# Zero fills of an attention-backward kernel as casting copies from an fp8 tile, issued by GpSimd

## The chip, the cores and the metric

The kernel runs on one core of a Trainium2 chip. The metric is the device time of one execution in microseconds (us). Engines are named as in the profile: PE is TensorE, DVE is VectorE, ACT is ScalarE, POOL is GpSimd and SP is SyncE. DMA transfers are carried by 16 DMA engines that all issuing engines share.

## The reference

One decode step of a transformer block and its gradients. A query of one token attends to the last 4096 of 32768 cached positions; the outputs hold the forward result and the gradients with regard to every input, the two whole caches among them.

```python
W = min(4096, max(256, Sk // 4))            # Sk = 32768: W = 4096
q = (x @ wq)                                # 16 heads of 256, 8 key/value heads
k = jnp.repeat(k_cache[:, :, Sk - W:, :], rep, axis=1)
v = jnp.repeat(v_cache[:, :, Sk - W:, :], rep, axis=1)
p = _softmax(jnp.einsum("bhqd,bhkd->bhqk", q, k) * (Dh ** -0.5), axis=-1)
a = jnp.einsum("bhqk,bhkd->bhqd", p, v)     # then @ wo
...
h = x + A(layernorm(x)); h2 = h + ((n @ w_gate) * (n @ w_up)) @ w_down   # n = layernorm(h)
...
_out, _vjp = jax.vjp(_f, A_x, A_k_cache, A_v_cache, A_wq, A_wo, B_w_gate, B_w_up, B_w_down)
```

The gradients of the caches (`out_2` for K, `out_3` for V) have the caches' shape, 8 x 32768 x 256 in bf16. Only the last 4096 positions of each head have a gradient; the other 28672 are zero, and the kernel has to write these zeros: 14.68 MB for each of 8 heads and 2 outputs, 234.9 MB in all.

## The kernel before, in words

The kernel is written with a tile framework that inserts the semaphores and chooses the order of the instructions on each engine; the order on an engine is fixed when the program is built, and each engine works its instructions off in that order. Two names choose the engine that issues transfers: `FILL` (SP before the change) for the zero fills and for the rows `x` and `grad_out`, and `IO` (POOL before the change) for all other loads and stores. The framework gives the transfers of each kind of issuer eight semaphores in turn, so a transfer that takes a semaphore again waits on its issuing engine until the one eight before it has landed.

The fills (lines 57 to 62): a tile `zeros` of 128 x 8192 bf16, 16 KB per partition, is cleared once by DVE, and 16 transfers copy it seven times each to the zero region of one head of one output, 128 x 7 rows of 16 KB.

The rest is one long chain of stages in which PE, DVE and ACT take part.

- Constants: POOL builds the two identity matrices `ident_bf` and `ident_f`, then `Par`, `Ed` and `Eq`. From `ident_f`, DVE works out `par`, `msk` (lines 112 to 117) and `mrow`.
- Head: `x` is put into columns and normalised; the normalised vector is multiplied with `msk` to give `xx` (line 188); 112 matmuls with `wq` (line 227) give `q`.
- Phase 1, eight groups g (lines 348 to 366), one per key/value head: load K and V of the window (`load_K`, `load_V`, line 79), scores with PE transposes (line 266), softmax, and `moments` (lines 308 to 334), whose matmuls need V and write to `MT` and `acc`. K and V lie in eight slots of 2 MB of one tile `S`; a load into a slot waits for the last reader of what was there. The first slots hold `wq`, so V loads into them wait for q.
- Middle: `wo` is loaded in two halves (`woA` at line 360, ahead of V of the last group's load in the queue; `woB` at line 375), `ao` is summed (line 382), then the gate and up projections, the second layernorm, the gradients down to `doT`, `dq_ps` (line 452) and `dq_bc`.
- Phase 2, eight groups g again (from line 559 on): V is transposed (line 567), `dp` is formed, and 32 matmuls per group (`d_ps`, line 601) give the gradient rows of V and K for the window. ACT and DVE take turns to copy them to staging slots of `S` (`evac`, lines 210 and 212), and two transfers of 2 MB per group store them (line 606). Between the groups stand side jobs: the outer products of the weight gradients (`outer`, lines 470 to 476), which DVE writes to two staging buffers in `Mt` and POOL stores, and the second reading of `wq` (lines 507 and 511).

Transfers of rows of 448 bf16 (896 B): `w_down` twice, `wo`, and the stores of the gradients of `wo` and `w_down`. All other large transfers on `IO` have rows of 2 KB and more.

Of the kernel before, what the change touches and what calls it, by code (L numbers as in the profile page):

```python
# [6 lines left out]

bf16 = mybir.dt.bfloat16
f32 = mybir.dt.float32
AX = mybir.AxisListType.X  # L10
ALU = mybir.AluOpType
ACT = mybir.ActivationFunctionType

D = 448
# [3 lines left out]
Dh = 256  # L18
W = 4096
# [3 lines left out]
Sk = 32768  # L23
# [4 lines left out]
NV = 5  # L28
HQ = H * Dh // 2
HF = F // 2  # L30
ZW = 8192
NZ = (Sk - W) * Dh // (128 * ZW)


K_SLOT = [5, 6, 7, 5, 6, 7, 5, 7]
# [5 lines left out]
def kernel(  # L41
        ctx, tc, A_x, A_k_cache, A_v_cache, A_wq, A_wo, B_x, B_w_gate, B_w_up, B_w_down, grad_out,
           out_0, out_1, out_2, out_3, out_4, out_5, out_6, out_7, out_8):
    nc = tc.nc
    V_, S_, P_ = nc.vector, nc.scalar, nc.tensor
    FILL = nc.sync
    IO = nc.gpsimd

    const = ctx.enter_context(tc.tile_pool(name="const", bufs=1))
    small = ctx.enter_context(tc.tile_pool(name="small", bufs=2))  # L50
    ps = ctx.enter_context(tc.tile_pool(name="ps", bufs=1, space=bass.MemoryType.PSUM))

    x_bf = const.tile([1, D], bf16, tag="rowa", name="x_bf")
    FILL.dma_start(out=x_bf[:], in_=A_x.rearrange("a b d -> (a b) d"))
    go_bf = const.tile([1, D], bf16, tag="rowb", name="go_bf")
    FILL.dma_start(out=go_bf[:], in_=grad_out.rearrange("a b d -> (a b) d"))
    zeros = const.tile([128, ZW], bf16)
    V_.memset(zeros[:], 0.0)
    for g in range(G):
        for o in (out_2, out_3):  # L60
            reg = o[0, g, 0:Sk - W, :].rearrange("s d -> (s d)").rearrange("(p n f) -> p n f", p=128, f=ZW)
            FILL.dma_start(out=reg, in_=zeros[:].unsqueeze(1).to_broadcast([128, NZ, ZW]))


    S = const.tile([128, NS, SLOT], bf16)
# [12 lines left out]
    def load_window(dst, cache, g):  # L78
        IO.dma_start(out=dst, in_=cache[0, g, Sk - W:, :].rearrange("(p t) d -> p t d", t=T))

    def load_K(g):
        load_window(Kw[g], A_k_cache, g)

    def load_V(g):
        load_window(Vw[g], A_v_cache, g)

    def flat_rows(w):
        return w.rearrange("a b -> (a b)").rearrange("(p x) -> p x", p=128)


    wq_sb = S[:, 1:3, :].rearrange("p a b -> p (a b)")[:, 0:NI * HQ]
    IO.dma_start(out=wq_sb, in_=flat_rows(A_wq))
    load_K(0)
    load_V(0)
    load_K(1)
    wd0 = S[:, 3, 0:FC * D].rearrange("p (c n) -> p c n", n=D)
    IO.dma_start(out=wd0, in_=B_w_down.rearrange("(c p) n -> p c n", p=128))

# [12 lines left out]
    par = const.tile([128, 2], f32)  # L111
    V_.reduce_sum(out=par[:, 1:2], in_=ident_f[:, 1::2], axis=AX)
    V_.tensor_scalar(out=par[:, 0:1], in0=par[:, 1:2], scalar1=-1.0, scalar2=1.0, op0=ALU.mult, op1=ALU.add)
# [54 lines left out]
    def layernorm(X, tag):  # L168
        s1 = small.tile([128, 1], f32, tag="ln_s")
        V_.reduce_sum(out=s1[:], in_=X, axis=AX)  # L170
        nm = small.tile([128, 1], f32, tag="ln_nm")
# [19 lines left out]
    def layernorm_bwd(Pp, xh, rstd, extra, gain, tag):  # L191

        st = small.tile([128, 2], f32, tag="lb_st")
        V_.reduce_sum(out=st[:, 0:1], in_=Pp, axis=AX)
        jk = small.tile([128, NI], f32, tag="lb_j")
# [87 lines left out]
    def softmax(g):  # L283
        s = sT[g]
        pmax = small.tile([128, 2], f32, tag="pmax")
        V_.reduce_max(out=pmax[:], in_=s[:].rearrange("p t h -> p h t"), axis=AX)
        mt = ps.tile([2, 128], f32, tag="tmp", bufs=1)
        P_.transpose(mt[:], pmax[:], ident_f[:])
        gmax = small.tile([2, 1], f32, tag="gmax")
        V_.reduce_max(out=gmax[:], in_=mt[:], axis=AX)  # L290
        gd = small.tile([2, 2], f32, tag="gd")
        V_.tensor_scalar(out=gd[:], in0=ident_f[0:2, 0:2], scalar1=gmax[:, 0:1], scalar2=-SCALE, op0=ALU.mult, op1=ALU.mult)
        nb = ps.tile([128, 2], f32, tag="tmp", bufs=1)
        P_.matmul(nb[:], lhsT=ones_f[0:2, :], rhs=gd[:], start=True, stop=True)
        nbias = small.tile([128, 2], f32, tag="nbias")
        V_.tensor_copy(out=nbias[:], in_=nb[:])
        e = small.tile([128, T, 2], f32, tag="e_f")
        sums = small.tile([128, 2], f32, tag="psums")
        for h in range(2):
            S_.activation(out=e[:, :, h], in_=s[:, :, h], func=ACT.Exp, bias=nbias[:, h:h + 1], scale=SCALE, accum_out=sums[:, h:h + 1])  # L300
        rs = small.tile([128, 2], f32, tag="rsum")
        V_.reciprocal(out=rs[:], in_=total(sums[:], 2)[:])
        pf = small.tile([128, T, 2], f32, tag="p_f")
        V_.tensor_tensor(out=pf[:], in0=e[:], in1=rs[:].unsqueeze(1).to_broadcast([128, T, 2]), op=ALU.mult)
        V_.tensor_copy(out=pT_all[:, g], in_=pf[:])
        p_f[g] = pf
# [41 lines left out]
    for g in range(G):  # L348
# [9 lines left out]
        if g == 7:  # L358
            load_V(7)
            IO.dma_start(out=woA, in_=wo_v[:, 0:16, :])  # L360
        softmax(g)
# [5 lines left out]
        if g == 0:  # L367
# [4 lines left out]
            for c in range(FC):  # L372
                V_.tensor_tensor_reduce(out=wd0[:, c, :], in0=wd0[:, c, :], in1=dh2_bc[:], scale=1.0, scalar=0.0,
                                        op0=ALU.mult, op1=ALU.add, accum_out=d_hh[:, c:c + 1])
    IO.dma_start(out=woB, in_=wo_v[:, 16:32, :])
    IO.dma_start(out=wg_sb, in_=flat_rows(B_w_gate))
    IO.dma_start(out=wu_sb, in_=flat_rows(B_w_up))
# [62 lines left out]
    pd = small.tile([128, H], f32, tag="pd")  # L440
    V_.reduce_sum(out=pd[:], in_=od[:].rearrange("p (h f) -> p h f", f=2), axis=AX)
    delta = const.tile([128, H], f32)
# [108 lines left out]
    rowb = late[:, 14336:16384].rearrange("p (k a c) -> p k a c", k=2, a=8)  # L551
# [7 lines left out]
    for g in range(G):  # L559
# [36 lines left out]
        for c in range(T // 2):  # L596
            d_ps = bps.tile([128, 2, 2, Dh], f32, tag="d2", bufs=2)
            for i in range(2):
                t = 2 * c + i
                k, a = t // 8, t % 8  # L600
# [38 lines left out]
```

## Time and profile before

| What | Value |
|---|---|
| time, median of 2 runs | 814.19 us (814.14 to 814.24) |
| span of the profiled execution | 812.7 us |
| bytes moved by DMA | 338.58 MB |
| HBM read, written | 57.28 MB, 280.59 MB |
| PE busy | 495.5 us (61%) |
| DVE busy | 374.0 us (46%) |
| ACT busy | 164.7 us (20%) |
| POOL busy | 40.5 us (5%) |
| q1 (SP's transfers) | 234.88 MB |
| q0 (POOL's transfers) | 103.00 MB |

How to read it: the span runs from the first to the last instruction of one profiled execution, and the medians come from runs of their own. Busy shares are averages over stages that differ. A row of 40 digits cuts the span in 40 equal slices (20.3 us each here), and a digit is a busy share in tenths, 9 for 90% and more. In a timeline line the first number is the start and the second the duration in us, then engine, line, operation, what is written and what is read; a bracket gives the idle time of the engine before it and what ended that. In a line of waits the numbers are the total in us, how often, and the longest. In the chain of waits each piece is start, duration and what the time was spent on.

### The profile page before, as it was taken

The page shows a single profiled execution, that of the slowest core. Times are in us where ns is not written, and L with a number is a line of the kernel's source. Part 1 is how long each engine was busy: PE and PEld are TensorE (multiplying, and loading weights), DVE is VectorE, ACT ScalarE, POOL GpSimd, SP SyncE. Part 2 cuts the span into 40 slices and gives each one's busy share as a digit, 9 for nine tenths or more (in the row PEclk, how much of TensorE's full clock was granted, in tenths as well). Part 3 has the DMA queues.
Part 4 walks back from the last instruction along what each step waited for, and adds up shares of the span by engine and source line. Part 5 has one row for each costly group of instructions (what it writes and reads, how often), then busy time and mean ns, then how long its engine had stood idle before and what let it go on. Part 6 is the DMA issues. An engine that isn't in the chain of part 4 may idle for free.

```text
span 812.7 us, 10923 instructions
## 1 busy us (share of the span) xinstructions
PE 495.5 (61%) x4479; PEld 289.6 (36%) x4479; DVE 374.0 (46%) x1149; ACT 164.7 (20%) x261; POOL 40.5 (5%) x75
## 2 busy tenths in 40 slices
PE   3559949999647519035497576099759674554500
PEld 3545636666223405013495432044325331210100
DVE  4128727777445306005671455366455435352500
ACT  0230101222000200001001233044435342332300
POOL 3000000000000001000000100001000001000000
PEclk9959778999678758655556555555555555555555
DMA  8999999999999999999999999999999999999994
GB/s 344 427 426 429 427 433 424 432 424 429 431 422 431 418 429 429 409 430 429 427 427 433 423 410 418 430 428 417 424 406 429 424 418 419 420 427 422 427 427 187
DMA packets 24567, 338.58 MB, mean 417 GB/s; under 512 B 1251, under 2 KB 1317, under 8 KB 4677
## 3 DMA queue, kind: packets, MB, share of 16 engines
q1 hardware_dynamic: 14596, 234.88, 68.4%
q0 software_dynamic: 9920, 103.00, 30.3%
q8 instruction: 35, 0.57, 0.3%
q14 instruction: 16, 0.12, 0.0%
HBM read 57.28 MB, written 280.59 MB: 416 GB/s over the span
## 4 chain that ended last, share of the span: by engine, by line
issue 29%; DMA 16%; PE 11%; DVE 4%; POOL 2%; ACT 1%; POOLq 0%; DVEq 0%
DMA S<-in_A_v_cache_dram 4%; DMA S<-in_A_wo_dram 4%; DMA Rt<-in_A_wq_dram 4%; DMA out_dram<-Mt 3%; PE dq_ps L452 3%; PE MT L322 2%; POOL out_dram L476 1%; DVE Rt L422 1%; POOL out_dram L606 1%; PE dh_ps L159 1%; PE d_ps L601 1%; PE tr L567 1%; PE t L412 1%; PE ao L382 1%; DVE Rt L511 1%
## 5 line engine op out<-in xcount | busy, mean ns | idle before, releaser
L601 PE MATMUL d_ps<-R,Mt 32*128 32x512 bf16 x256 | 124.4, 613 | 92.4 <-DVE S L212 91.6
L322 PE MATMUL MT<-Rt,S 128*128 128x512 bf16 x512 | 145.9, 397 | 30.7 <-DMA S<-in_A_v_cache_dram 29.8
L318 DVE TENSOR_SCALAR Rt<-S,pf 128x256 bf16<-128x256 bf16 x512 | 117.0, 281 | 56.4 <-PE MT L322 49.7
L212 DVE CAST S<-d_ps 128x512 bf16<-128x512 f32 x128 | 86.7, 688 | 55.5 <-ACT S L210 44.0
L210 ACT CAST S<-d_ps 128x512 bf16<-128x512 f32 x128 | 75.0, 586 | 169.8 <-PE d_ps L601 169.8
L601 PEld LDWEIGHTS <-Mt 32*128 32x128 bf16 x256 | 23.3, 114 | 146.1 <-issue 144.7
L567 PE MATMUL tr<-ident_bf,S 128*128 128x128 bf16 x512 | 69.6, 306 | 3.5 <-ACT Mt L210 3.5
L325 PEld LDWEIGHTS <-S 128*128 128x128 bf16 x512 | 49.4, 100 | 60.9 <-issue 9.5
L266 PE MATMUL tr<-ident_bf,S 128*128 128x128 bf16 x512 | 48.6, 253 | 36.4 <-DMA S<-in_A_k_cache_dram 32.0
L567 PEld LDWEIGHTS <-S 128*128 128x128 bf16 x512 | 49.2, 137 | 28.0 <-issue 27.8
L266 PEld LDWEIGHTS <-S 128*128 128x128 bf16 x512 | 38.1, 115 | 34.7 <-DMA S<-in_A_k_cache_dram 32.3
L325 PE MATMUL acc<-pT_all,S 128*128 128x2 bf16 x512 | 48.2, 166 | 0.0
L328 PE MATMUL acc<-pT_all,S 128*128 128x2 bf16 x512 | 47.5, 164 | 0.0
L322 PEld LDWEIGHTS <-S 128*128 128x128 bf16 x512 | 33.5, 98 | 36.7 <-DMA S<-in_A_v_cache_dram 30.7
L210 ACT COPY Rt<-tr 128x1024 bf16<-128x1024 bf16 x32 | 32.4, 1012 | 67.2 <-PE tr L266 66.9
L210 ACT COPY Mt<-tr 128x1024 bf16<-128x1024 bf16 x32 | 32.4, 1014 | 56.6 <-PE tr L567 29.5
L330 ACT COPY Mt<-MT 128x512 f32<-128x512 f32 x8 | 4.7, 585 | 192.3 <-PE MT L322 164.3
L382 PE MATMUL ao<-S,oT_bf 128*1 128x448 bf16 x32 | 9.6, 468 | 45.9 <-DMA S<-in_A_wo_dram 45.9
L212 DVE COPY Rt<-tr 128x1024 bf16<-128x1024 bf16 x32 | 22.0, 688 | 32.7 <-PE tr L266 31.8
L572 PEld LDWEIGHTS <-Mt 128*128 128x128 bf16 x512 | 20.0, 108 | 37.0 <-DVE Mt L212 14.0
L328 PEld LDWEIGHTS <-S 128*128 128x128 bf16 x512 | 30.9, 97 | 0.1
L572 PE MATMUL dp<-doT,Mt 128*128 128x2 bf16 x512 | 22.6, 168 | 12.6 <-DVE Mt L212 10.8
(182 smaller groups left out, 454.5 us busy)
## 6 DMA issues: line engine op xcount, KB each, us to landing
out_dram<-zeros SPq DMA_DIRECT2D x16, 14336.0 KB, 148.2
out_dram<-S POOLq DMA_DIRECT2D x16, 2048.0 KB, 29.3
S<-in_A_v_cache_dram POOLq DMA_DIRECT2D x11, 2048.0 KB, 36.3
S<-in_A_k_cache_dram POOLq DMA_DIRECT2D x8, 2048.0 KB, 29.0
out_dram<-Mt POOLq DMA_DIRECT2D x6, 896.0 KB, 22.2
S<-in_A_wq_dram POOLq DMA_DIRECT2D x1, 3584.0 KB, 14.8
S<-in_A_wo_dram POOLq DMA_DIRECT2D x2, 1792.0 KB, 31.8
out_dram<-Mt POOLq DMA_DIRECT2D x3, 1024.0 KB, 34.0
```

The source lines that it names most:

```text
L210: S_.copy(out=out, in_=in_)
L212: V_.tensor_copy(out=out, in_=in_)
L266: P_.transpose(tr[:, i, dh, :], Xw[:, 4 * q + i, dh * 128:(dh + 1) * 128], ident_bf[:])
L318: V_.tensor_scalar(out=pk[:, i, h, :], in0=K[:, t, :], scalar1=pf[:, t, h:h + 1], scalar2=None, op0=ALU.mult)
L322: P_.matmul(MT[:, hf, :], lhsT=Vv[:, t, hf * 128:(hf + 1) * 128], rhs=pk[:, i, :, :].rearrange("p h d -> p (h d)"), start=(t == 0), stop=( ...
L325: P_.matmul(acc[:, 2 * hf:2 * hf + 2], lhsT=Vv[:, t, hf * 128:(hf + 1) * 128], rhs=pT_all[:, g, t, :], start=(t == 0 and hf == 0), stop=(t ...
L328: P_.matmul(acc[:, 4 + dk:7 + dk:2], lhsT=K[:, t, dk * 128:(dk + 1) * 128], rhs=pT_all[:, g, t, :], start=False, stop=(t == T - 1), skip_g ...
L382: P_.matmul(ao[:], lhsT=oT_bf[:, b:b + 1], rhs=wo_b(b), start=(b == 0), stop=(b == 31))
L452: P_.matmul(dq_ps[:, 2 * h + dk:2 * h + dk + 1], lhsT=Mt[:, h // 2, hf, c0:c0 + 128], rhs=doT_f[:, 2 * h + hf:2 * h + hf + 1], start=(hf = ...
L567: P_.transpose(tr[:, i, dh, :], Vw[g][:, 4 * q + i, dh * 128:(dh + 1) * 128], ident_bf[:])
L572: P_.matmul(dp[:, 4 * q + i, :], lhsT=xt[:, i, dh, :], rhs=doT[:, 4 * g + dh:4 * g + dh + 3:2], start=(dh == 0), stop=(dh == 1))
L601: P_.matmul(d_ps[:, i, :, :].rearrange("p w d -> p (w d)"), lhsT=rows[32 * k:32 * k + 32, a, :], rhs=R[32 * k:32 * k + 32, :], start=True, ...
```

## The change

The fills move from SP to POOL, and all other transfers, `x` and `grad_out` among them, from POOL to SP. The zero tile becomes 7 KB per partition, declared as 1792 f32 so that it can be cleared in words of four bytes, and is read by the fills as 7168 elements of fp8 (`float8e4`). The zero region of the output is viewed as f32, in four rows of 7168 elements (28 KB) for each of 128 partitions. Since the types differ, each fill is a copy that converts fp8 zeros to f32 zeros; four zero bytes of f32 are two zeros of bf16.

```diff
+f8 = mybir.dt.float8e4
...
-ZW = 8192
-NZ = (Sk - W) * Dh // (128 * ZW)
+ZR = (Sk - W) * Dh // 256
+ZW = 7168
+NZ = ZR // ZW
...
-    FILL = nc.sync
-    IO = nc.gpsimd
+    FILL = nc.gpsimd
+    IO = nc.sync
...
-    x_bf = const.tile([1, D], bf16, tag="rowa", name="x_bf")
-    FILL.dma_start(out=x_bf[:], in_=A_x.rearrange("a b d -> (a b) d"))
-    go_bf = const.tile([1, D], bf16, tag="rowb", name="go_bf")
-    FILL.dma_start(out=go_bf[:], in_=grad_out.rearrange("a b d -> (a b) d"))
-    zeros = const.tile([128, ZW], bf16)
+    zeros = const.tile([128, ZW // 4], f32)
     V_.memset(zeros[:], 0.0)
     for g in range(G):
         for o in (out_2, out_3):
-            reg = o[0, g, 0:Sk - W, :].rearrange("s d -> (s d)").rearrange("(p n f) -> p n f", p=128, f=ZW)
-            FILL.dma_start(out=reg, in_=zeros[:].unsqueeze(1).to_broadcast([128, NZ, ZW]))
+            reg = o[0, g, 0:Sk - W, :].rearrange("s d -> (s d)").rearrange("(p n f) -> p n f", p=128, n=NZ).bitcast(f32)
+            FILL.dma_start(out=reg, in_=zeros[:].bitcast(f8).unsqueeze(1).to_broadcast([128, NZ, ZW]))
...
+    x_bf = const.tile([1, D], bf16, tag="rowa", name="x_bf")
+    IO.dma_start(out=x_bf[:], in_=A_x.rearrange("a b d -> (a b) d"))
+    go_bf = const.tile([1, D], bf16, tag="rowb", name="go_bf")
+    IO.dma_start(out=go_bf[:], in_=grad_out.rearrange("a b d -> (a b) d"))
```

In the built program the instructions of POOL then stand in this order: the clearing of both identity matrices, the affine_select that completes `ident_bf`, fills 1 to 8, fills 9 to 16 (each with a wait for the semaphore of the fill eight before it), the affine_select that completes `ident_f`, and `Par`, `Ed` and `Eq`. On SP stand first x, grad_out, wq, K0, V0, K1, w_down, K2 and V4 (into slots that nothing held), then the V loads that wait for q's matmuls, and the rest in the order in which POOL had them. On PE some transposes of K move ahead of the matmuls of q; DVE and ACT keep their orders but for a few copies.

## The prediction

> **What bounds the kernel now.** I read the page's DMA rows first, then the share of each queue stretch by stretch, then the chain of waits, then the timelines of SP and POOL.
>
> ```profile
> DMA  8999999999999999999999999999999999999994
> GB/s 344 427 426 429 427 433 424 432 424 429 431 422 431 418 429 429 409 430 429 427 427 433 423 410 418 430 428 417 424 406 429 424 418 419 420 427 422 427 427 187
> DMA packets 24567, 338.58 MB, mean 417 GB/s; under 512 B 1251, under 2 KB 1317, under 8 KB 4677
> ...
> q1 hardware_dynamic: 14596, 234.88, 68.4%
> q0 software_dynamic: 9920, 103.00, 30.3%
> ```
>
> The DMA engines are full from the second slice to the last but one, at about 427 GB/s. The queues' shares by stretch change (SP's fills have 52% in the first 100 us, 87% from 300 to 400, 61% from 600 to 700), loads and stores change places beside them, and the sum stays there. 338.58 MB at 427 GB/s is 793 us of a span of 812.7: the bytes bound the kernel. q1 is SP's queue: 16 fills of 128x7 rows are 14336 of its 14596 packets, so on it a row is a packet. A packet takes 0.684 x 812.7 x 16 / 14596 = 0.609 us for 16 KB, or 26.9 GB/s per engine. q0 is POOL's. 13568 rows of 896 B are moved on it (w_down twice, wo, o5, o8), and 4677 - 1317 = 3360 of its packets are between 2 and 8 KB: about four such rows share a packet of 3.5 KB (0.133 us).
>
> ```profile
> 5.25 0.29 POOL masks.py:199 TENSOR_SCALAR_AFFINE_SELECT ident_f<-ident_f 128x128 f32<-128x128 f32 x1
> ...
> 15.46 0.21 DVE L112 TENSOR_REDUCE par<-ident_f 128x1 f32<-128x64 f32 x1
> ...
> 16.81 0.17 DVE L188 TENSOR_TENSOR xx<-xf,msk 128x14 bf16<-128x14 f32 x1
> ...
> 27.79 3.17 PE L227 MATMUL q_ps<-xx,S 128*128 128x2 bf16 x112
> ...
> 31.18 1.61 POOL L79 DMA_DIRECT2D S<-in_A_v_cache_dram  x3 [22.84 <-PE q_ps L227]
> ...
> 265.55 1.18 POOL L360 DMA_DIRECT2D S<-in_A_wo_dram  x1 [32.27 <-PE acc L325]
> ...
> 769.89 0.53 POOL L606 DMA_DIRECT2D out_dram<-S  x1 [0.19 <-issue]
> ```
>
> In the timeline the head of the compute is a thin line: ident_f (POOL) -> par -> msk -> xx (DVE) -> q_ps (PE). Without ident_f there is no q, and without q no scores, no softmax and no free slot for the next loads. From q (31 us) to the last issue of a store (769.9) it runs beside the fills. SP's 16 issues of fills are strung from 5.2 to 630.7 us, because each of the later ones waits until a fill eight semaphores earlier has landed; behind them SP has nothing else to do.
>
> ```profile
> 267.73 36.30 DMA S<-in_A_v_cache_dram
> ...
> 321.97 35.62 DMA S<-in_A_wo_dram
> ...
> 433.79 12.61 DMA out_dram<-Mt
> ...
> 455.09 15.26 DMA out_dram<-Mt
> ...
> 491.89 29.78 DMA Rt<-in_A_wq_dram
> ```
>
> These pieces of the chain show what compute pays for full DMA engines. Over 530 to 813 us the waits add:
>
> ```profile
> DVE Mt L475 <- DMA out_dram<-Mt: 54.9, 7, 12.2
> ...
> DVE S L212 <- DMA out_dram<-S: 10.9, 2, 7.1
> ```
>
> **The change, part by part.**
>
> *The fills' rate.* 16 fills still write 14.68 MB each to HBM, 234.9 MB; from SBUF they draw a quarter of that. The trace has no casting transfer. Nearest rows: an engine passes 26.9 GB/s in fills (q1), and 0.303 x 812.7 x 16 us for 103 MB, 26.1 GB/s, in POOL's mix, whose loads write SBUF and read HBM. A rate that is the same in both directions and does not rise when they mix belongs to the engine or to HBM's side, and the output still crosses both at full width. I take 427 GB/s of written bytes. Upper end: four times that, if only source bytes count. Lower end: half, if converting doubles a byte's time.
>
> The Trainium skill speaks for the high side: its "DMA: Bandwidth & Descriptors", section "Where 436 GB/s comes from", calls the 16 SBUF ports the bottleneck, which casting relieves. But the same page, section "Latency and other measured facts", gives 214 GB/s per direction as the full rate of copies from HBM to HBM: HBM's side then carries 428 in all, and casting spares nothing. No run here shows which; by the second the sum below stands, by the first the second rival does.
>
> *The order on POOL.* In the built program the fills stand on POOL between the affine_select of ident_bf and that of ident_f. Fills 1 to 8 go out at once; 9 to 16 wait for fills 1 to 8, one each; ident_f, Par, Ed and Eq stand behind all of them. So ident_f is built when fill 8 has landed, not at 5.25 us. SP's first loads (x, go, wq, K0, V0, K1, w_down, K2, V4: 3.67 + 5 x 2.10 + 1.61 = 15.8 MB) go out meanwhile; the next V waits for q's matmuls, and with it everything behind on SP.
>
> 1. The smaller memset ends at 1.67 + 3.47 x 1792/4096 = 3.2 us. Fill 8 lands at 3.2 + (8 x 14.68 + 15.8)/0.427 = 315 us.
> 2. ident_f to xx to q_ps to qT: 0.3 + 1.5 + 3.3 + 0.2, so q is there at 320, where it was at 31.
> 3. From q to the issue of wo's first half the trace has 265.6 - 31.2 = 234 us. K0's second part and K1 lie ready, which takes off 9.4 and 10.5 of waiting: 214. Issue at 535.
> 4. Fills 9 to 16 run meanwhile; all fills and the 38.3 MB of loads up to here end at 3.2 + (234.9 + 38.3)/0.427 = 643. Before that, wo meets them: 128 rows of 896 B per engine, on SP's queue a packet each, taking turns with 28 KB packets of 1.07 us: 128 x 1.1 = 141 us, beyond the fills' end, and V7 is queued behind wo. V7 lands at about 650. Where rows go four to a packet instead, 32 x 1.2 + 8 x 1.68 = 52 us: V7 at 587. (The same sum for before, 32 x 0.74 + 8 x 1.22 = 33.5, stands against 38.5 measured.) I take a row per packet, as in SP's own rows.
> 5. From V7 to the end before: 812.7 - 304.0 = 508.7. The fills are gone, so: wo's second half 35.6 -> 8 (saves 27.6); the three DMA pieces of 12.6, 15.3 and 29.8 -> 4, 4 and 6 (0.9 to 1.6 MB at 427 GB/s, 2 us added as my estimate; saves 43.7); of the 65.8 us that DVE waits for DMA after 530, between 0 and 66, and I take two thirds, 44, since in the d_ps loop DVE and ACT alternate; the drain after the last issue, 42.3, becomes 4.7 MB/0.427 + 2 = 13 (saves 29). Sum 144; 364 remain.
> 6. 650 + 364 = 1014. The profiled span of before, 812.7, lies 1.5 below its median of 814.19: **1016 us**.
>
> Bounds at this rate: V7 at 587 then pays 18 of moments and 38 for wo's second half, and from ao on has 455 - 117 = 338 left: 983; with all 66 saved, 961. With none of the 44 and an SP queue that holds stores back as it held fills, 1060. The memset's 2 us and the reordered transposes ahead of q (DVE and PE idle there) cost nothing: they lie within the 300 us in which both wait. That cover cannot go unless fill 8 lands before about 30 us. x and go, on SP ahead of wq, land long before ident_f. POOL no longer issues loads and stores (0.53 us each); SP does, and nothing else is on it.
>
> **Rivals.**
>
> *Hidden anyway.* The bytes are the same, and compute could catch up once ident_f is there. At 315 us, 205 MB are left, 481 us: 796 at best, about as before. Against it: from q on before takes 781 us, and the waits for DMA that the trace names (20 + 46 before wo, 39, 35, 66, and the drain's 29) are 235. Without all of them 546 remain, and 320 + 546 = 866. At 427 GB/s nothing ends under that.
>
> *The cast lifts the rate.* If SBUF's ports are the limit, fills pass rate R. By steps 4 to 6 the fills end at 3.2 + 90 + 234.9/R, V7 comes 7 later, and 366 follow: 814 where R is 0.68 MB/us, 1.6 times today's; with every DMA wait gone, at 1.23 times. Twice: fill 8 at 178, V7's issue at 397, V7 at 405, end about 770. Four times: 690 to 710. For it: the sum of 427 does not tell which port it belongs to. Against it: stores and loads load different directions of SBUF's ports and do not add up to more. The Trainium skill's "HBM Reference", section "Specifications", gives 716 GB/s per domain; at that rate the sum would be about 806, no change, and no run here shows such a rate.
>
> *The cast is slower.* At half rate the fills alone last to 3.2 + 90 + 1100 = 1193, and 372 follow: 1565; at 0.8 times, 1155. Nothing in the trace shows it or excludes it.
>
> *The order does not bind,* if POOL passes the waits early: then 338.6 MB at 427 bound it, 800 to 820.
>
> **How the numbers follow.** Forecast (rate as now, POOL held until fill 8): 0.62, 960 to 1060. Cast slower than 0.9 times: 0.15, above 1060. Cast faster: 0.20, spread from 690 to 960, of which 0.12 under 798, 0.04 within 2% of 814, 0.04 above. Order not binding: 0.03, no change. Faster by over 2% (about what a measurement of this kernel can tell from no change) 0.12, within 2% 0.07, slower 0.81. For eight in ten the range goes down to 800, leaving out the 0.12 below, and up to 1160, where the half-rate cast (0.08) lies outside. The likeliest case's own range is 960 to 1060.
>
> **What would show it.** In the changed profile: the POOL timeline with ident_f at 300 us or later, behind the sixteenth fill; PE and DVE idle from about 10 us until then; DMA full to about 640, in the rows of the 40 slices, and then well below 9; V7's load and both wo loads slow while fills run; the GB/s row at 427 in the first third. If that row stands at 600 or more, the cast has moved the limit and the second rival holds; if it is under 390, the third. If ident_f comes before 50 us, my reading of the order is wrong. If the fills leave early and the time still is above 1000, step 5 is wrong, and compute alone is longer than I read.

## The result and the profile after

The changed kernel takes 1010.01 us (median; 1009.43 to 1010.6) against 814.19 before: ratio 1.2405, 95% interval 1.2369 to 1.2441. The profiled execution spans 1008.8 us, so a slice of the 40 is 25.2 us here. The source lines below the fills stand two lines further down than before (L227 is now L229, L360 is L362).

The page of the changed kernel, its rows of slices and its queues:

```profile
PE   2100000000001789674940707676498789899973
...
DMA  9999999999999999999999999640205555633576
GB/s 378 427 433 424 422 432 431 424 436 437 434 433 427 428 428 429 431 431 428 430 433 432 435 427 432 238 169 33 64 1 196 198 225 228 250 153 142 240 323 260
DMA packets 29146, 338.58 MB, mean 336 GB/s; under 512 B 1188, under 2 KB 14760, under 8 KB 15400
...
q0 software_dynamic: 8448, 234.88, 55.4%
q1 hardware_dynamic: 20648, 103.00, 38.2%
```

The GB/s row has two halves. For 25 slices it stands at about 427, as before, and the same bytes move; then it falls to 33, 64 and 1 and never fills again. PE does next to nothing until 317 us and is busy at the end: work that ran beside the fills now runs after them. q0 is now POOL's queue with the fills, q1 SP's with the rest. The packets under 2 KB rose from 1317 to 14760.

POOL's timeline in the changed kernel: the eight fills issued at once, the first and the last of the eight that had to wait, and what stands behind them:

```profile
3.06 6.00 POOL L60 DMA_DIRECT2D out_dram<-zeros  x8 [1.65 <-DVE eps_t L111]
62.05 0.71 POOL L60 DMA_DIRECT2D out_dram<-zeros  x1 [52.99 <-DMA out_dram<-zeros]
...
314.25 0.71 POOL L60 DMA_DIRECT2D out_dram<-zeros  x1 [33.14 <-DMA out_dram<-zeros]
314.89 0.38 POOL masks.py:199 TENSOR_SCALAR_AFFINE_SELECT ident_f<-ident_f 128x128 f32<-128x128 f32 x1
```

And the timeline of all engines right behind it:

```profile
317.41 0.15 DVE L190 TENSOR_TENSOR xx<-xf,msk 128x14 bf16<-128x14 f32 x1
317.61 3.13 PE L229 MATMUL q_ps<-xx,S 128*128 128x2 bf16 x112 [279.02 <-DVE xx L190]
...
320.78 0.19 DVE L231 CAST qT<-q_ps 128x32 bf16<-128x32 f32 x1 [3.22 <-PE q_ps L229]
```

`ident_f` stands behind the sixteenth fill, and each waiting issue is let go by a landed fill: PE waits 279 us for `xx`. The last three of these issues stand 33.7 to 33.9 us apart, with next to no other traffic: 14.68 MB in 33.8 us is 434 GB/s of written bytes, and beside loads the row stands at about 427.

SP's timeline in the changed kernel (SPq is SP's issuing, its waits included):

```profile
101.72 219.78 SPq L77 DMA_DIRECT2D S<-in_A_v_cache_dram  x3
...
623.34 0.38 SPq L362 DMA_DIRECT2D S<-in_A_wo_dram  x1
625.53 19.29 SPq L77 DMA_DIRECT2D S<-in_A_v_cache_dram  x1
670.10 0.38 SPq L377 DMA_DIRECT2D S<-in_A_wo_dram  x1
...
996.65 1.06 SPq L608 DMA_DIRECT2D out_dram<-S  x2
```

The last load of V in phase 1 (V7 below; K7 is the last of K) lands 28.9 us after its issue, at 654.4. In the stretch from 640 to 650 us the fills have 2.1% of the DMA engines left: they end there. Behind V7 come 354 us, and from 730 us on neither PE, DVE nor ACT waits for a DMA.

The queues of the changed kernel from 610 to 620 us:

```profile
q1 hardware_dynamic: 84, 1.11, 193.8%
q0 software_dynamic: 112, 3.21, 76.4%
```

This pair looks odd and is worth learning to read: 84 packets of SP's queue are on record for 1.938 x 10 us x 16 engines = 310 us, 3.7 us each, while a 28 KB packet of the fills next to them takes 0.764 x 160 / 112 = 1.09 us. Records overlap, so the share passes 100%, and the mean hides two kinds: the 68 packets of data, 16 KB each, take 0.65 to 0.70 us, and 16 writes of 4 bytes take 14.8 to 19.1 us each, 265 of the 310 us. These are the writes with which the load of K7 announces on each DMA engine that it is complete. The last of them ends at 636.1, and PE starts on K7 at 636.5; the experiments follow such writes up.

### The profile page after: what moved, and what is told of

Same layout as the page of the kernel before. It is cut to its first block, busy times and chain, and to the rows that moved or that the text cites. A ratio compares the mean times of both kernels' runs of the same rounds, so it can differ in the third digit from the quotient of the medians.

```text
span 1008.8 us, 10891 instructions
## 1 busy us (share of the span) xinstructions
PE 498.7 (49%) x4445; PEld 295.3 (29%) x4479; DVE 374.0 (37%) x1149; ACT 164.9 (16%) x261; POOL 14.8 (1%) x31
## 3 DMA queue, kind: packets, MB, share of 16 engines
q1 hardware_dynamic: 20648, 103.00, 38.2%
## 4 chain that ended last, share of the span: by engine, by line
PE 41%; another core or an unknown queue 33%; DMA 8%; issue 6%; DVE 6%; ACT 4%; POOL 1%; POOLq 0%; ACTq 0%; DVEq 0%
PE MT L324 10%; PE d_ps L603 9%; PE tr L569 6%; DMA S<-in_A_k_cache_dram 4%; PE tr L268 3%; PE dq_ps L454 3%; DMA S<-in_A_v_cache_dram 3%; DVE S L214 2%; ACT S L212 2%; PE dp L574 2%; PE sT L273 1%; PE acc L327 1%; PE acc L330 1%; DMA S<-in_A_wo_dram 1%
## 5 line engine op out<-in xcount | busy, mean ns | idle before, releaser
L324 PE MATMUL MT<-Rt,S 128*128 128x512 bf16 x478 | 138.2, 394 | 56.1 <-DMA S<-in_A_v_cache_dram 55.3
L229 PE MATMUL q_ps<-xx,S 128*128 128x2 bf16 x112 | 3.1, 166 | 279.0 <-DVE xx L190 279.0
L268 PE MATMUL tr<-ident_bf,S 128*128 128x128 bf16 x512 | 56.5, 281 | 75.3 <-DMA S<-in_A_k_cache_dram 70.9
L229 PEld LDWEIGHTS <-S 128*128 128x128 bf16 x112 | 3.1, 104 | 279.1 <-issue 279.1
L569 PE MATMUL tr<-ident_bf,S 128*128 128x128 bf16 x512 | 68.7, 303 | 3.9 <-ACT Mt L212 3.9
L268 PEld LDWEIGHTS <-S 128*128 128x128 bf16 x512 | 45.3, 130 | 74.4 <-DMA S<-in_A_k_cache_dram 71.7
L327 PEld LDWEIGHTS <-S 128*128 128x128 bf16 x512 | 49.2, 100 | 60.9 <-issue 8.8
L569 PEld LDWEIGHTS <-S 128*128 128x128 bf16 x512 | 48.3, 135 | 27.2 <-issue 26.9
L324 PEld LDWEIGHTS <-S 128*128 128x128 bf16 x512 | 33.5, 98 | 61.7 <-DMA S<-in_A_v_cache_dram 55.8
L330 PEld LDWEIGHTS <-S 128*128 128x128 bf16 x512 | 30.9, 97 | 3.4 <-issue 3.4
## 6 DMA issues: line engine op xcount, KB each, us to landing
S<-in_A_wq_dram SPq DMA_DIRECT2D x1, 3584.0 KB, 17.8
S<-in_A_wo_dram SPq DMA_DIRECT2D x2, 1792.0 KB, 11.4
```

What stands on the lines that cost most here:

```text
L268: P_.transpose(tr[:, i, dh, :], Xw[:, 4 * q + i, dh * 128:(dh + 1) * 128], ident_bf[:])
L324: P_.matmul(MT[:, hf, :], lhsT=Vv[:, t, hf * 128:(hf + 1) * 128], rhs=pk[:, i, :, :].rearrange("p h d -> p (h d)"), start=(t == 0), stop=( ...
L327: P_.matmul(acc[:, 2 * hf:2 * hf + 2], lhsT=Vv[:, t, hf * 128:(hf + 1) * 128], rhs=pT_all[:, g, t, :], start=(t == 0 and hf == 0), stop=(t ...
L330: P_.matmul(acc[:, 4 + dk:7 + dk:2], lhsT=K[:, t, dk * 128:(dk + 1) * 128], rhs=pT_all[:, g, t, :], start=False, stop=(t == T - 1), skip_g ...
L569: P_.transpose(tr[:, i, dh, :], Vw[g][:, 4 * q + i, dh * 128:(dh + 1) * 128], ident_bf[:])
```

## The experiments

Theory at the start ("order theory"): the fills ahead of `ident_f` on POOL hold the head of the chain for 315 us, and this sets the time. Rivals: the loads, now on SP's queue with a row per packet, get too small a share beside the fills' long rows ("share" or "turn" theory), or the cast itself is at fault ("cast theory"; later, in the form that casting copies hold other transfers' completions, "hold theory"). "Constants first" means that the block with `zeros` and the fills is moved in the source behind the identities, `Par`, `Ed` and `Eq`, so that POOL builds these first; the diffs of such kernels leave the move out below. All ratios are to the kernel before, with 95% intervals.

### The order alone

masks_first: constants first, casting fills of 28 KB rows kept.

```diff
-    zeros = const.tile([128, ZW // 4], f32)
-    V_.memset(zeros[:], 0.0)
-    for g in range(G):
-        for o in (out_2, out_3):
...
     S = const.tile([128, NS, SLOT], bf16)
...
+    zeros = const.tile([128, ZW // 4], f32)
+    V_.memset(zeros[:], 0.0)
+    for g in range(G):
+        for o in (out_2, out_3):
...
```

> The changed kernel with the fill block moved behind the constants in the source, so that POOL builds ident_f, Par, Ed and Eq before the first fill; casts, rows and queues stay. Order theory (the time was lost because ident_f stood behind fills 9 to 16): q is there at about 30 us as before the change, the bytes bound again, 800 to 840 us. Share theory (SP's loads and stores get too little beside the fills of 28 KB rows, whenever q comes: phase 1 took 303 us from q to wo's issue with fills beside it, 234 before the change): phase 1 lasts to 330 or later, wo and the last V load come late, and the time is 880 to 1000 us. Cast theory (converting costs DMA time): above 1000 us.

Measured: 1010.97 us, ratio 1.2426 (1.2403 to 1.2448). The order theory falls as the sole cause: with `ident_f` early again, nothing is won. The number lies where the cast theory had put it, but the trace shows more than one thing. SP's timeline in this kernel (the line that loads K and V is L69 here):

```profile
457.84 0.38 SPq L362 DMA_DIRECT2D S<-in_A_wo_dram  x1
460.02 69.15 SPq L69 DMA_DIRECT2D S<-in_A_v_cache_dram  x1
```

and PE, when V7 has come:

```profile
649.72 1.03 PE L324 MATMUL MT<-Rt,S 128*128 128x512 bf16 x2 [36.06 <-DMA S<-in_A_v_cache_dram]
```

`wo` is issued 165 us earlier than in the changed kernel, and V7 still comes at the same time: its load takes 189.7 us, until the fills leave. The rest, 1003.3 - 649.7 = 353.6 us, is the changed kernel's 354. Two different delays, the late head and the slow loads, end at the same place, the fills' end, and so undoing one alone shows nothing. The queues of masks_first from 110 to 130 us, while `w_down` loads, show the share:

```profile
q0 software_dynamic: 288, 8.26, 96.8%
q1 hardware_dynamic: 291, 0.26, 7.6%
```

288 packets of fills against 291 of loads: one packet each in turn. A turn brings the fills 28 KB and the loads 896 B, and SP's queue gets 0.26 MB in 20 us, 13 GB/s.

### Plain fills, in both orders

plain_blocked: bf16 zeros without a cast in rows of 8 KB (`ZW` 4096), `ident_f` still behind the fills. masks_first_plain: constants first, plain rows of 16 KB (`ZW` 8192). (With a plain tile of 16 KB the framework puts the fills behind `ident_f` by itself, hence the 8 KB.)

```diff
-    zeros = const.tile([128, ZW // 4], f32)
+    zeros = const.tile([128, ZW], bf16)
...
-            FILL.dma_start(out=reg, in_=zeros[:].bitcast(f8).unsqueeze(1).to_broadcast([128, NZ, ZW]))
+            FILL.dma_start(out=reg, in_=zeros[:].unsqueeze(1).to_broadcast([128, NZ, ZW]))
```

> The changed kernel with plain bf16 copies from a bf16 tile of 8 KB per partition in rows of 8 KB; the order on POOL, with ident_f behind the sixteenth fill, and the queues stay. Order theory: ident_f at 305 to 325 us and a time within 3% of the changed kernel's 1010 us. Cast theory: under 900 us. Share theory: phase 1 is faster by smaller packets, but the fills end at the same time of about 635 us, so 950 to 1010 us.

> Constants first on POOL as in the run with the constants ahead of the fills, and plain bf16 fills of 16 KB rows from the 16 KB tile of before, issued by POOL; loads and stores on SP. It differs from the kernel before only in which queue carries which transfers. Order theory: 800 to 840 us. Share theory: packets of 16 KB in place of 28 KB give SP's transfers more, so between the kernel before and the run with casting fills, 830 to 930 us. Cast theory: 814 us, and clearly under the run with casting fills.

Measured: plain_blocked 988.79 us (1.2149, 1.2115 to 1.2182), masks_first_plain 902.31 us (1.1078, 1.1062 to 1.1095). Neither order nor cast is the whole: without both, 88 us over before are left.

### The cast the other way

narrow_cast: the changed kernel with f32 zeros written as bf16, rows of 8 KB written and 16 KB read.

```diff
-ZW = 7168
+ZW = 4096
...
-    zeros = const.tile([128, ZW // 4], f32)
+    zeros = const.tile([128, ZW], f32)
...
-            FILL.dma_start(out=reg, in_=zeros[:].bitcast(f8).unsqueeze(1).to_broadcast([128, NZ, ZW]))
+            FILL.dma_start(out=reg, in_=zeros[:].unsqueeze(1).to_broadcast([128, NZ, ZW]))
```

> The changed kernel with the cast the other way round: fills convert an f32 zero tile of 16 KB per partition to bf16 rows of 8 KB, so that twice the written bytes are read from SBUF. The order on POOL stays blocked. If HBM's side sets the fills' rate (written bytes count), a fill takes 33 to 35 us once it is alone, ident_f comes at 305 to 325 us and the time stays near 1010 us. If an engine's pace goes by the wider side of a copy, a fill takes 67 to 70 us, ident_f comes at 590 us or later and the time is 1500 us or more.

Measured: 1446.42 us (one time, without an interval), somewhat under the 1500 expected for a pace that goes by the wider side. Its page:

```profile
GB/s 301 245 222 275 215 217 216 214 214 212 213 213 213 212 213 213 232 280 270 253 264 256 234 222 240 248 221 222 240 219 222 241 267 238 245 255 143 222 285 247
```

While fills run alone, 213 GB/s are written and so 427 read, and `ident_f` comes at 595 us. With the changed kernel (427 written, 107 read) this says: these casting copies go at the pace of their wider side.

### Shorter rows under the cast

first_cast16k and first_cast8k: masks_first with `ZW` 4096 and 2048, so rows of 16 and 8 KB.

```diff
-ZW = 7168
+ZW = 4096
```

> Constants first on POOL, casting fills as in the change but in rows of 16 KB from a tile of 4 KB per partition, so that only the cast separates it from the run with plain fills of 16 KB rows (902.3 us). If the cast itself neither saves nor costs anything, 893 to 911 us. If converting costs DMA time of its own, above 920; if sparing SBUF reads helps, under 885. Turn theory (each engine takes a packet of SP's queue and a packet of POOL's in turn, so the fill's row length sets what SP gets): the same 902.

> Constants first, casting fills in rows of 8 KB. Turn theory: a turn of the fills is 0.30 us in place of 1.07 (28 KB) and 0.61 (16 KB), w_down's 112 rows per engine take about 40 us beside the fills and wo's 128 about 45, so phase 1 is near that of before, and the time falls on from 1011 and 902 to 800 to 850 us. If the row length does not matter and it is the mere order of the bytes, it stays above 900.

Measured: 984.82 us (1.2092, 1.2076 to 1.2109) and 907.12 us (1.1137, 1.112 to 1.1154). Shorter rows help, 1011 to 985 to 907, but the cast stays dear: at 16 KB it is 82.5 us slower than plain fills in the same order and with the same rows (902.31), and at 8 KB 83.1 us (907.12 against 823.98 in first_plain8k below). So the turn theory, which had 800 to 850 for 8 KB, is right for plain fills and misses the casting ones. The loads of K and their queue, first in first_cast16k:

```profile
q1 hardware_dynamic: 20648, 103.00, 43.4%
...
S<-in_A_k_cache_dram SPq DMA_DIRECT2D x8, 2048.0 KB, 50.7
```

then in masks_first_plain:

```profile
q1 hardware_dynamic: 20648, 103.00, 28.1%
...
S<-in_A_k_cache_dram SPq DMA_DIRECT2D x8, 2048.0 KB, 19.3
```

The same 20648 packets with the same bytes are on record for 0.434 x 982.6 x 16 = 6823 us beside the cast and 0.281 x 900.4 x 16 = 4048 us beside plain fills, and K takes 50.7 us to land (the median of 8 loads) in place of 19.3. The trace's records of single packets say which: not the data, for the most part, but the completion write of 4 bytes. Beside plain fills such a write takes 9 ns (median) on SP's queue, and the 932 of them 8 us in sum. In first_cast16k they sum to 2395 us, most of the 2775 us of difference: 112 take over 2 us ("held" below), the longest 31.2, and 103 of these end within 0.3 us of the completion write of a fill. In first_cast8k 138 take over 2 us, the longest 33.8. By the records the data of a load has been moved, and the engine that waits for it is told so up to a whole fill later.

### Splitting the casting fills

first_cast16k_split: each fill as seven transfers of one row per partition, so that fills complete seven times as often.

```diff
-            FILL.dma_start(out=reg, in_=zeros[:].bitcast(f8).unsqueeze(1).to_broadcast([128, NZ, ZW]))
+            for n in range(NZ):
+                FILL.dma_start(out=reg[:, n, :], in_=zeros[:].bitcast(f8))
```

> Constants first, casting fills of 16 KB rows, but each fill split into seven transfers of one row per partition, so that an engine works at 8 packets of a casting transfer in place of 56 until its semaphore write. In the casting runs the trace holds the 4-byte completion writes of SP's loads for up to 31 us, until the fill under way on that engine ends (985 us against 902 for plain fills of the same rows). Hold theory: the hold can last 5 us at most, K and V land in 15 to 25 us, and the time falls to 895 to 925 us. If the difference between cast and plain comes from the packets themselves, it stays at 965 to 1000.

Measured: 921.06 us (1.131, 1.1291 to 1.1329), 64 of the 82.5 us back. The longest completion write is now 4.6 us, their sum 467 us, and the queue and K's loads:

```profile
q1 hardware_dynamic: 20648, 103.00, 33.4%
...
S<-in_A_k_cache_dram SPq DMA_DIRECT2D x8, 2048.0 KB, 26.6
```

The hold theory holds: bytes, rows and order are those of first_cast16k, and fills complete more often. The edit also leaves less in flight, eight transfers of 2.1 MB in place of eight of 14.7, but the records point at the completions: these fall by 1928 us in sum, and the record time of the whole queue by 1910.

The split leaves a second effect of the cast, which the records show and no experiment takes alone. For transfers issued after nothing of SP's queue had moved for 3 us, the first packet starts 0.5 to 0.7 us after the issue once the fills are gone. Beside plain and narrowing fills it starts 3.1 to 3.4 us after it (medians of five kernels), beside widening ones 8.6 to 10.6 us (medians of seven), and in this run 10.3, so the split does not help there. It may be what is left of the 82.5 us.

### Long rows on SP's queue

first_wide: masks_first, with `w_down` (twice), `wo` and the stores of their gradients in long rows. This pairs the rows of these weights and gradients with other partitions than the reference does.

```diff
-    IO.dma_start(out=wd0, in_=B_w_down.rearrange("(c p) n -> p c n", p=128))
+    IO.dma_start(out=wd0, in_=B_w_down.rearrange("(p c) n -> p c n", p=128))
...
-    wo_v = A_wo.rearrange("(b p) n -> p b n", p=128)
+    wo_v = A_wo.rearrange("(p b) n -> p b n", p=128)
```

> Constants first, casting fills of 28 KB rows as in the change; w_down (twice), wo and the stores of the gradients of wo and w_down have their rows assigned to the partitions in blocks, so that each partition moves one long row in place of rows of 896 B. This puts rows of the weights and gradients in other places than the reference, and changes no byte count and no instruction count on the engines. Turn theory: w_down lands before 80 us (181 before), wo and the V load behind it within 30 us (190 before), and the time is 820 to 890 us. Theory that the 28 KB fills starve every transfer alike: above 950.

Measured: 898.49 us (1.1031, 1.1016 to 1.1046), 112 us under masks_first and a little over the 890 that the turn theory allowed; the held writes remain here (127 over 2 us). The first load of `w_down`, in masks_first:

```profile
S<-in_B_w_down_dram SPq DMA_DIRECT2D x1, 1568.0 KB, 181.2
```

and in first_wide:

```profile
S<-in_B_w_down_dram SPq DMA_DIRECT2D x1, 1568.0 KB, 72.7
```

Before the change it took 63.3 us on POOL's queue with the short rows.

first_plain16k_wide: masks_first_plain with the same long rows (the same edit).

> Constants first, plain fills of 16 KB rows on POOL (902.3 us), and the transfers with rows of 896 B given long rows, which puts rows of the weights and gradients in other places than the reference and leaves all counts and bytes. Row theory: what is left between 902 and the 814 of before is SP's moving one 896 B row per turn, so 810 to 830 us. If moving the other transfers to SP costs by itself, above 850.

Measured: 812.01 us (0.9971, 0.996 to 0.9982), 90 us under masks_first_plain. Its page:

```profile
GB/s 337 430 430 428 428 428 430 426 427 431 428 430 426 429 425 429 429 426 428 433 413 425 418 433 421 429 422 430 429 427 430 428 426 426 426 428 429 431 428 146
```

The DMA engines are full to the last slice but one: here the bytes bound the kernel again, as before.

### Row length without a cast

first_plain8k: masks_first_plain with `ZW = 4096`. before_8k: the kernel before with the same edit, whose loads stay on POOL.

```diff
-ZW = 8192
+ZW = 4096
```

> Constants first and plain fills in rows of 8 KB on POOL; it differs from the run with plain 8 KB fills and ident_f behind them (988.8 us) only in the order on POOL. Order theory: with no cast and a short turn the late ident_f is what is left of that run's loss, so 830 to 880 us here. If the order costs nothing here either, as with the casting fills of 28 KB (1011 against 1010), it is above 970.

> The kernel before with its plain fills on SP in rows of 8 KB in place of 16 KB, nothing else. Turn theory: loads and stores get more beside the fills, compute is done earlier and the fills end last; the bytes bound stays at 793 us plus some 10 at the ends, so 800 to 812 us, unless the shorter rows cost the DMA engines their pace (the plain fills of 8 KB rows ran at about 422 GB/s against 428), which makes 810 to 822.

Measured: first_plain8k 823.98 us (1.0116, 1.0098 to 1.0134), 78 us under the 16 KB rows; before_8k 819.06 us (1.0054, 1.0041 to 1.0067). Where loads have their share anyway, shorter rows cost 5 us; where the loads take turns row by row, they bring 78. And first_plain8k against plain_blocked, the same fills with `ident_f` behind them, shows what the order costs once it alone is late: 988.79 - 823.98 = 165 us, where it cost nothing at 28 KB.

### All mended, cast kept

cast_all_mended: constants first, casting rows of 16 KB, split, long rows on SP.

> The casting fills with all that was found undone: constants first, rows of 16 KB, each fill split in seven transfers, and the transfers with rows of 896 B given long rows (rows of the weights and gradients in other places than the reference, all counts and bytes kept). If the cast brings and costs nothing beyond the four causes, it stands within 2% of the same kernel with plain fills (812.0): 805 to 828. If the cast raises the DMA engines' rate once nothing else binds, under 795. If a cost of the cast remains, 830 or more.

Measured: 817.32 us (1.0035, 1.0022 to 1.0047). Its page:

```profile
GB/s 366 427 424 422 430 425 427 429 425 428 429 429 428 426 429 428 427 429 430 429 430 430 427 425 426 432 426 428 426 427 426 425 424 428 424 428 427 427 399 37
```

With these side effects taken away or cut short the cast gains nothing, and it costs 5.3 us against the same kernel with plain fills (812.01): the slow first packets are left, and completion writes of up to 4.3 us. Walked back from here, each step undoing one remedy, 193 of the 196 us of the change are found again: short rows on SP +103.7 (to 921.06), unsplit fills +63.8 (984.82), 28 KB rows +26.2 (1010.97), `ident_f` behind the fills -1.0 (1010.01), which is within the scatter of masks_first (1005 to 1014). The terms overlap, so another sequence of steps gives others: the order is worth 0 in this one and 165 us in the plain 8 KB kernels.

## Why the prediction came out right, point by point

The predicted 1016 us lie 6 over the measured 1010.01, and the forecast case is the one that occurred. Not all of its reasons stand, and that the number is so close is in part luck: 88 us that step 3 missed are swallowed because the last loads of phase 1 come with the fills' end either way, and behind them other misses cancel in part.

- *The fills' rate*: as taken, 427 GB/s of written bytes beside loads, 434 alone. The rivals of a faster and a slower cast fall with the first 25 slices. The Trainium skill's "DMA: Bandwidth & Descriptors", section "Where 436 GB/s comes from", makes the SBUF ports the limit; the trace doesn't bear out that sparing three quarters of their reads gains anything (427 with and without). A limit on HBM's side alone doesn't fit either, since narrow_cast writes it at 213. A limit in the DMA engine, or equal ones on both sides, would give both numbers; no run here separates these. (The last sum of the rival of a faster cast, 806 us, is 796 by its own terms; nothing hangs on it, since the rate stayed.)
- *Steps 1 and 2* (fill 8, then q): `ident_f` at 314.9 against 315, qT at 320.8 to 321.0 against 320. Right.
- *Step 3* (214 us from q to `wo`'s first half): failed, 623.3 - 321.0 = 302. The working took over the pace of phase 1 from the trace of before. In the changed kernel its loads are late. PE's waits for them between 318 and 625 us:

```profile
PE MT L324 <- DMA S<-in_A_v_cache_dram: 55.3, 2, 31.4
...
PE tr L268 <- DMA S<-in_A_k_cache_dram: 38.1, 3, 12.8
```

  These are 93.4 us, where the sum had left 22.4 (42.3 before, less the 19.9 it took off); that is 71 of the 88. Four of the five waits, 69.5 us together, are held completions almost in full: the completion writes of the load begin before PE asks for it or within 2 us after, most of them last 13 to 31 us, and PE goes on within 0.9 us of the end of the last. The fifth, 23.9 us for V6, has no write over 2 us: its first packet starts 10.6 us after its issue, and then it takes turns with packets of 28 KB. The other 17 us were not followed up. plain_blocked, with q as late but plain fills of 8 KB rows, took 528.9 - 328.6 = 200 us for this step, so it is the casting fills and their long rows that the sum lacked. That a row is a packet on SP was foreseen, but applied to `wo` alone.
- *Step 4* (V7 at 650): 654.4, right in number by another way. `wo`'s 141 us were to begin at 535 and carry V7 past the fills' end; `wo` was issued only at 623, its first row started at 632.7, and it never met more than the tail of the fills. PE hardly waited for V7 (0.8 us in its weight loads). What stands before that in the chain is K7, told of only when the last fills leave, and behind it the scores, the softmax and the first matmuls of `ao`, which end at 654.65:

```profile
636.51 1.89 PE L268 MATMUL tr<-ident_bf,S 128*128 128x128 bf16 x16 [11.02 <-DMA S<-in_A_k_cache_dram]
```

  masks_first shows the forecast mechanism in the open: issue at 458, V7 189.7 us later. Its row per packet is confirmed by the 13572 packets between 512 B and 2 KB, up from 66, which are the 13568 rows of 896 B. (On POOL's queue before, it was five rows to a packet, 2624 packets of 4480 B, and not about four: the 3360 packets that were counted hold other transfers too.)
- *Step 5* (364 us behind V7): 354. `wo`'s second half took 11.4 us where 8 were put, the drain after the last issue 12 against 13; DVE's waits for DMA in phase 2 went altogether, 66 where 44 were taken, and so did the three pieces of the chain that were put at 4, 4 and 6. These sizes make 34 us less, where 10 were measured; what took the other 24 was not found.
- *That the order on POOL is the cause*: wrong as the sole cause, though it is a fact of the profile, and worth 165 us where the loads are fast (plain_blocked against first_plain8k). Put right alone it brings nothing (masks_first), because the turns (and with them the held completions) keep V7 to the fills' end too. The rival "the order does not bind" was priced at 800 to 820 because it was thought to be the only thing in the way; with the order not binding the time is 1011.
- *"Hidden anyway"*: no run contradicts the argument that at least 546 us of work remain behind q. plain_blocked, with q as late and K's loads among the fastest (17.8 us in the median), ended at 985.0 in its span, 656 behind q (328.6).

Why it is exactly widening copies that hold completions, and delay first packets, stays open. The Trainium skill, "DMA: Bandwidth & Descriptors", section "Queues, rings and completion order", says that the increment of a semaphore is a strongly ordered write, which lands only after every earlier write of that DMA engine, those of other queues too. The 31 us agree with that, but by that sentence alone plain fills and narrowing casts would hold as well, and beside both no completion took over 0.1 us. In the changed kernel only 33 of its 91 held writes end with a fill's own completion; what lets the others go was not found.

## What to carry to other kernels

When bulk writes and loads that compute waits for share the DMA engines, look at what a packet is on each queue and count turns, not bytes: a queue whose packets are 896 B long got 13 GB/s beside packets of 28 KB. A stall that is plain in the timeline is the cause only if the time falls when it alone is taken away; if two delays both end with the fills, neither shows until the other is gone, so ask of each term what would be late next. A narrower source gains nothing where the pace goes by the wider side, and it may cost others: look at the completion writes and the first packets of the loads beside a casting copy, and split long casting copies into short transfers.

## What the runs showed of the hardware

- Beside a widening casting copy (fp8 to f32) the completion writes of another queue were held up to 33.8 us (first_cast8k), beside 16 KB rows up to 31.2 us and beside the same copy split in seven up to 4.6 us; beside plain and narrowing copies none passed 0.1 us, and beside plain ones the median is 9 ns.
- On an SP queue that had been still for 3 us, the first packet started 0.5 to 0.7 us after the issue with no fills, 3.1 to 3.4 us beside plain or narrowing fills, and 8.6 to 10.6 us beside widening ones (medians of kernels).
- A casting copy kept 427 GB/s or a little more on its wider side: 427 to 434 written when widening, 213 written when narrowing to half.
- SP's queue moved 896 B rows one to a packet and in turn, 291 packets to 288, with rows of 28 KB; on POOL's queue before, five such rows shared a packet, and `w_down` landed in 63 us in place of 181. The Trainium skill, "DMA: Bandwidth & Descriptors", section "Queues, rings and completion order", has the queues take turns by packets, which the trace bears out, and 9 to 17 descriptors in a typical packet; on SP's queue the packets were single rows.
- No version that computes the whole reference was found that is faster than before. Its bytes at 427 GB/s take 793 us, so at most 2.6% were left to win.
